# A second gated layer by seven block products instead of eight, with the output product moved behind it

## The chip, the cores and the metric

The kernel runs on one core of one Trainium2 chip. The metric is device time in microseconds (us). TensorE (PE, with its weight loads as PEld) multiplies into PSUM, which has eight banks here; VectorE (DVE) and ScalarE (ACT) read PSUM and work in SBUF; GpSimd (POOL) works in SBUF; SyncE (SP) issues DMAs.

## What is computed

```python
x = attention(q, k, v)                    # 2 x 768 tokens -> 1536 x 512
h = ((x @ moe_w1) * (x @ moe_w2)) @ moe_w3
y = h @ moe_w_out                         # 1536 x 512
a = y @ moe2_w_a                          # 512 x 1536
b = y @ moe2_w_b                          # 512 x 1536
return ((a * b) @ moe2_w_out).astype(np.float32)   # 1536 x 512
```

All inputs are float32 except the weights of both layers, which arrive as 64-bit floats and are turned into 32-bit ones on the chip.

## The kernel before

Tokens are the columns of the matmuls: 1536 tokens are three groups of `TG = 512`. Every 32-bit operand is held as two rounded parts (`fp32r`), hi and lo, and a product is three matmuls, lo·hi, hi·lo and hi·hi (`product`, L122 to L128, and `gate`, L679 to L681). A contraction of 512 is four chunks of 128, so a gate of one weight block and one token group is 12 matmuls into one PSUM bank.

The program is emitted by a generator, engine by engine, in the order of the text; nothing reorders it afterwards, and each engine works through its own queue in that order. Attention and the first layer's gates come first, mixed. Then `moe` (L693) makes y in twelve products of 24 matmuls (tags `y`, L736 to L756): three token groups of four row chunks each; ACT copies the hi part out of PSUM and DVE subtracts it for lo (`split_psum`, L77). At the same time ACT and DVE split the operands of the next group (`split_g`, L701).

The second layer's 1536 features are twelve blocks f of 128. For each f and token group, `gate` (L671) makes a and b in two banks (24 matmuls), ACT copies b out (L686), DVE multiplies (L687), and `split_sbuf` (L689) splits the result. The output product runs between the gates: features are taken in six groups of two, and `out_piece` (L765) multiplies a group's two blocks for one tile of 128 tokens (six matmuls) and adds the bank to an accumulator in SBUF (L786). The pieces of the last group follow the last gate; the last tile is done in two halves of 256 columns.

Weights come through `feed` (L180): SP loads a 512 KB block, ACT rewrites its two words (L94, L95), DVE joins them in three steps (L101, L105, L109), ACT rounds (L113), DVE subtracts (L117). Tiles come from pools with a fixed number of buffers (`unit` 34, `half` 8, `late` 11, PSUM `bank` 8), so a new tile waits for the last reader of the buffer that it takes.

Of the kernel before, what the change touches and what calls it, by code (L numbers as in the profile page):

```python
# [8 lines left out]
F32 = mybir.dt.float32  # L9
F32R = mybir.dt.float32r  # L10
I32 = mybir.dt.int32
# [3 lines left out]
ALU = mybir.AluOpType  # L15

P = 128
TG = 512
# [9 lines left out]
def f32(ap):  # L28
    return ap.bitcast(F32)


class Emitter:
# [48 lines left out]
    def convert(self, hi, lo, raw):  # L81
# [5 lines left out]
        g = self.half("g", list(hi.shape))  # L87
        gi = g.bitcast(I32)

        def words():  # L90

            nc.scalar.activation(out=g, in_=f32(high), func=AF.Copy, scale=WORD_SCALE)  # L94
            nc.scalar.activation(out=low, in_=low.bitcast(U32), func=AF.Copy, scale=2.0**-29)  # L95
            yield

        def join():


            nc.vector.tensor_scalar(  # L101
                out=gi, in0=gi, scalar1=0x0FFFFFFF, scalar2=3, op0=ALU.bitwise_and, op1=ALU.logical_shift_left
            )
# [6 lines left out]
            yield  # L110

        def upper():
# [18 lines left out]
    def weight_jobs(self):  # L131

        io, C = self.io, self.C
        nk = self.NF1
        wide, square = [P, 1, 2 * self.DM], [P, C, 2 * P]
        jobs = []
        for what, f, *_ in self.order:
            if what == "fold":
                for k in range(0, nk if f == 0 else 0, 2):
                    jobs.append((("wo", k), [(io["moe_w_out"][k + j].unsqueeze(1), wide) for j in range(2)]))  # L140
                jobs.append((("w3", f), [(io["moe_w3"][f][:, g : g + 4, :], square) for g in range(0, nk, 4)]))
            elif all(key != ("w12", f) for key, _ in jobs):
                jobs.append((("w12", f), [(io[n][f], square) for n in ("moe_w1", "moe_w2")]))
        for f in range(self.NF2):
            jobs.append((("wab", f), [(io[n][f], square) for n in ("moe2_w_a", "moe2_w_b")]))
            if f:
                jobs.append((("wo2", f - 1), [(io["moe2_w_out"][f - 1].unsqueeze(1), wide)]))
        jobs.append((("wo2", self.NF2 - 1), [(io["moe2_w_out"][self.NF2 - 1].unsqueeze(1), wide)]))
        return jobs

    def feed_start(self):
# [541 lines left out]
    def moe(self):  # L693

        nc, io = self.nc, self.io
        nf = self.NF1
# [1 line left out]
        g1 = [{} for _ in range(self.NTG)]  # L698
        gs = [[] for _ in range(self.NTG)]

        def split_g(tg, f):  # L701
            t = self.unit("gs", [P, 2, TG], F32R)
            self.split_sbuf(t, g1[tg].pop(f))
            gs[tg].append(t)

# [24 lines left out]
                    split_g(0, e)  # L730
            yield 1.3 * (at.stop - at.start) / TG

        self.lead = 6
        y = []
        nf2 = self.NF2
        for tg in range(self.NTG):  # L736
            ys = []
            for n in range(self.C):
                p = self.bank("y")
                cols = slice(n * P, (n + 1) * P)  # L740
                self.product(
# [3 lines left out]
                        for f in range(nf)  # L745
                    ],
                )
                t = self.act("y")
                self.split_psum(t[:, 0, :], t[:, 1, :], p)
                ys.append(t)  # L750
                if tg + 1 < self.NTG:
                    for f in range(2 * n, 2 * n + 2):
                        split_g(tg + 1, f)
                yield 5.2
            y.append(ys)
            gs[tg] = None  # L756
        self.wf = None

        ntt = self.NT // P
        acc = [self.late("acc", [P, 2, self.DM]) for _ in range(ntt // 2)]  # L760
        outs, g2 = {}, {}
        FG = 2
        groups = nf2 // FG

        def out_piece(grp, tt):  # L765
            for f in range(grp * FG, (grp + 1) * FG):
                if f not in outs:
                    outs[f] = self.need("wo2", f)[0]
            tg, o = divmod(tt * P, TG)
            a = acc[tt // 2][:, tt % 2, :]  # L770

            parts = 2 if (grp, tt) == (groups - 1, ntt - 1) else 1
            for n in range(parts):
                at = slice(n * self.DM // parts, (n + 1) * self.DM // parts)
                p = self.bank("o", (P, self.DM // parts))
                self.product(
                    p,
                    [
                        (g2[f][tg][:, 0, o : o + P], g2[f][tg][:, 1, o : o + P], outs[f][:, 0, 0, at], outs[f][:, 1, 0, at])
                        for f in range(grp * FG, (grp + 1) * FG)  # L780
                    ],
                )
                if grp == 0:
                    nc.vector.tensor_copy(out=a[:, at], in_=p)
                else:
                    nc.vector.tensor_tensor(out=a[:, at], in0=a[:, at], in1=p, op=ALU.add)  # L786
                if grp == groups - 1:
                    nc.sync.dma_start(io["out"][tt * P : (tt + 1) * P, at], a[:, at])

        for grp in range(groups):  # L790
            todo = [(grp - 1, tt) for tt in range(ntt)] if grp else []
            per = -(-ntt // (FG * self.NTG))
            for f in range(grp * FG, (grp + 1) * FG):
                g2[f] = []
                pair = self.need("wab", f)
                for tg in range(self.NTG):
                    g = self.half("gg", [P, TG])
                    yield from self.gate(pair, lambda c, tg=tg: (y[tg][c][:, 0, :], y[tg][c][:, 1, :]), g)
                    t = self.unit("g2", [P, 2, TG], F32R)
                    self.split_sbuf(t, g)  # L800
                    g2[f].append(t)
                    for _ in range(per):
                        if todo:
                            out_piece(*todo.pop(0))
                    yield 1.3
        for tt in range(ntt):
            out_piece(groups - 1, tt)
            yield 1.3

    def finish(self, work):  # L810
# [5 lines left out]
def tile_kernel(ctx, tc, io):  # L816
# [34 lines left out]
        e.hp, e.up = e.pool("hp", 8), e.pool("up", 34)  # L851
        return e

    def rest(e):
        e.lp = e.pool("lp", 11)

    with tc.If(narrow) as branch:
        with ExitStack() as arm, tc.manual_schedule():
# [6 lines left out]
            rest(e)  # L865
            e.finish(work)
    with branch.Else():
        with ExitStack() as arm, tc.manual_schedule():
            e = emitter(arm, "full")
            with ExitStack() as ctx:  # L870
                e.const, e.lp = e.pool("const", 1, ctx), e.pool("ap", 10, ctx)
                e.full_attention()
            rest(e)
            e.feed_start()
            e.finish(e.moe())

# [58 lines left out]
```

## Time and profile before

| | |
|---|---|
| three runs | 631.29, 632.20, 632.98 us; median 632.2 |
| profiled execution, first to last instruction | 631.2 us (its own time beyond this span is not listed) |
| PE busy | 614.2 us, 97% |
| DVE busy | 386.2 us, 61% |
| ACT busy | 299.1 us, 47% |
| POOL busy | 74.5 us, 12%, all of it in the first 130 us |
| chain that ended last | PE 87%, DVE 7%, ACT 2% |
| y products | from 267.2 us to 332.4 us |
| second layer's gates and the output product | from 332.4 us to 626.4 us |

Busy time is the time in which an engine had an instruction in flight; neighbouring matmuls overlap, so the distance from one start to the next, not the duration of one, is what a matmul costs. The chain follows the last instruction back through whatever released it.

### The profile page before, as it was taken

What the parts mean: (1) busy time and instruction counts of PE and PEld (TensorE: products, weight loads), DVE (VectorE), ACT (ScalarE), POOL (GpSimd) and SP (SyncE); (2) the same over time, 40 slices, a digit from 0 to 9 for tenths busy, and PEclk for the clock granted to TensorE, in tenths of its full rate; (3) what the DMA queues carried; (4) which work ended last, traced back from release to release, by engine and by line L of the source; (5) the groups of instructions that cost most, each with busy time, mean ns of one, the idle gap of its engine ahead of it and who ended that gap; (6) DMA issues with size and microseconds to landing.
All of it is one profiled execution on the core that took longest, in us unless ns stands there. A gap on an engine that the chain in (4) does not pass through costs nothing.

```text
span 631.2 us, 8920 instructions
## 1 busy us (share of the span) xinstructions
PE 614.2 (97%) x3230; PEld 512.0 (81%) x3230; DVE 386.2 (61%) x866; ACT 299.1 (47%) x655; POOL 74.5 (12%) x122
## 2 busy tenths in 40 slices
PE   6999999999999999999999999999999999999996
PEld 4688988888888888888888888888888888888885
DVE  6897989369874985823315566466566556553344
ACT  5898899656563774622314453153253243331110
POOL 5665667300000000000000000000000000000000
PEclk9899999999999999999999999999999999999999
DMA  8999772335331650100014011112112111000004
GB/s 233 270 256 210 174 195 68 135 126 174 106 128 34 199 175 25 69 1 0 1 36 165 33 34 67 67 66 68 68 66 67 67 67 66 1 0 1 0 35 171
DMA packets 20276, 58.86 MB, mean 93 GB/s; under 512 B 2688, under 2 KB 3456, under 8 KB 20224
## 3 DMA queue, kind: packets, MB, share of 16 engines
q1 hardware_dynamic: 19648, 57.42, 30.4%
q10 hardware_dynamic: 576, 0.79, 0.5%
q8 instruction: 27, 0.44, 0.3%
q14 instruction: 25, 0.20, 0.1%
HBM read 55.05 MB, written 3.15 MB: 92 GB/s over the span
## 4 chain that ended last, share of the span: by engine, by line
PE 87%; DVE 7%; ACT 2%; issue 2%; DMA 1%; POOL 1%; POOLq 0%; DVEq 0%; ACTq 0%
PE ab_band L679 16%; PE ab_band L681 16%; PE ab_band L680 16%; PE o_band L127 5%; PE o_band L128 5%; PE o_band L126 5%; PE y_band L128 3%; PE y_band L126 3%; PE y_band L127 3%; PE wfp_band L246 2%; PE wfp_band L248 2%; PE wfp_band L247 2%; PE pv_band L526 2%; DVE s_band L454 2%; PE pt_band L490 2%
## 5 line engine op out<-in xcount | busy, mean ns | idle before, releaser
L680 PE MATMUL ab_band<-y_band,w_band 128*128 128x512 f32 x288 | 112.0, 389 | 0.0
L679 PE MATMUL ab_band<-y_band,w_band 128*128 128x512 f32 x288 | 112.0, 389 | 0.0
L681 PE MATMUL ab_band<-y_band,w_band 128*128 128x512 f32 x288 | 112.0, 389 | 0.0
L686 ACT COPY b_band<-ab_band 128x512 f32<-128x512 f32 (+1 forms) x63 | 35.5, 566 | 150.7 <-PE ab_band L681 150.6
L679 PE MATMUL ab_band<-xh_band,w_band 128*128 128x512 f32 (+1 forms) x216 | 81.8, 379 | 0.0
L687 DVE TENSOR_TENSOR gg_band<-ab_band,b_band 128x512 f32<-128x512 f32 x36 | 24.9, 691 | 92.3 <-ACT b_band L686 92.3
L681 PE MATMUL ab_band<-xh_band,w_band 128*128 128x512 f32 (+1 forms) x216 | 79.0, 366 | 0.0
L680 PE MATMUL ab_band<-xl_band,w_band 128*128 128x512 f32 (+1 forms) x216 | 78.9, 365 | 0.0
L113 ACT CAST w_band<-g_band 128x512 fp32r<-128x512 f32 x76 | 47.3, 622 | 47.2 <-DVE g_band L109 45.0
L479 POOL TENSOR_SCALAR s_band<-s_band,z_band 128x256 f32<-128x256 f32 (+1 forms) x96 | 61.0, 648 | 37.1 <-DVE z_band L477 16.7
L679 PEld LDWEIGHTS ab_band<-y_band,w_band 128*128 128x128 f32 x288 | 54.1, 188 | 11.3
L680 PEld LDWEIGHTS ab_band<-y_band,w_band 128*128 128x128 f32 x288 | 54.1, 188 | 11.2
L681 PEld LDWEIGHTS ab_band<-y_band,w_band 128*128 128x128 f32 x288 | 54.1, 188 | 11.1
L109 DVE CUSTOM_DVE_ANT_0 g_band<-raw_band,g_band 128x1024 uint16<-128x1024 uint16 x76 | 52.9, 696 | 10.3 <-ACT raw_band L95 0.5
L127 PE MATMUL o_band<-w_band,g_band 128*128 128x512 f32 (+1 forms) x146 | 56.4, 386 | 0.0
L126 PE MATMUL o_band<-w_band,g_band 128*128 128x512 f32 (+1 forms) x146 | 56.4, 386 | 0.0
L128 PE MATMUL o_band<-w_band,g_band 128*128 128x512 f32 (+1 forms) x146 | 56.4, 386 | 0.0
L105 DVE SCALAR_TENSOR_TENSOR g_band<-raw_band,g_band 128x512 int32<-128x512 int32 x76 | 52.5, 691 | 2.3
L117 DVE TENSOR_TENSOR w_band<-g_band,w_band 128x512 fp32r<-128x512 f32 x76 | 51.2, 690 | 3.9 <-ACT w_band L113 3.5
L94 ACT ACTIVATE g_band<-raw_band 128x512 f32<-128x512 f32 x76 | 50.9, 670 | 0.0
L95 ACT ACTIVATE raw_band<-raw_band 128x512 int32<-128x512 uint32 x76 | 50.7, 668 | 0.0
L466 ACT ACTIVATE s_band<-s_band,m_band 128x256 f32<-128x256 f32 (+1 forms) x96 | 46.6, 492 | 3.5 <-DVE m_band L454 3.4
(89 smaller groups left out, 1036.0 us busy)
## 6 DMA issues: line engine op xcount, KB each, us to landing
raw_band<-in_moe_w_dram SPq DMA_DIRECT2D x31, 512.0 KB, 4.6
raw_band<-in_moe_w_out_dram SPq DMA_DIRECT2D x20, 512.0 KB, 4.2
raw_band<-in_moe_w_a_dram SPq DMA_DIRECT2D x12, 512.0 KB, 3.7
raw_band<-in_moe_w_b_dram SPq DMA_DIRECT2D x12, 512.0 KB, 3.7
v_band<-in_v_dram SPq DMA_DIRECT2D x12, 256.0 KB, 8.1
kd_band<-in_kq_dram SPq DMA_DIRECT2D x12, 256.0 KB, 7.5
qd_band<-in_kq_dram SPq DMA_DIRECT2D x12, 256.0 KB, 7.7
out_dram<-acc_band SPq DMA_DIRECT2D x11, 256.0 KB, 2.0
```

The source lines that it names most:

```text
L94: nc.scalar.activation(out=g, in_=f32(high), func=AF.Copy, scale=WORD_SCALE)
L95: nc.scalar.activation(out=low, in_=low.bitcast(U32), func=AF.Copy, scale=2.0**-29)
L105: nc.vector.scalar_tensor_tensor(out=gi, in0=high, scalar=-0x80000000, in1=gi, op0=ALU.bitwise_and, op1=ALU.bitwise_or)
L109: nc.vector.tensor_tensor(out=gi, in0=gi, in1=low, op=ALU.add)
L117: nc.vector.tensor_tensor(out=lo, in0=g, in1=f32(hi), op=ALU.subtract)
L126: self.nc.tensor.matmul(out, wl, xh, start=(i == 0), stop=False)
L127: self.nc.tensor.matmul(out, wh, xl, start=False, stop=False)
L128: self.nc.tensor.matmul(out, wh, xh, start=False, stop=(i == n - 1))
L479: nc.gpsimd.tensor_scalar(out=s[:, j, lo:], in0=s[:, j, lo:], scalar1=z[:, j : j + 1], scalar2=1.0, op0=ALU.mult, op1=ALU.mult)
L679: nc.tensor.matmul(p, wl, xh, start=(c == 0), stop=False)
L680: nc.tensor.matmul(p, wh, xl, start=False, stop=False)
L681: nc.tensor.matmul(p, wh, xh, start=False, stop=(c == self.C - 1))
```

## The change

The 2 x 2 blocks are: two halves of the contraction (256 each), the pair of weight blocks (w_a, w_b) of one f, and two halves of the tokens. Instead of eight block products of 256, seven are made (Strassen's algorithm in Winograd's form), from sums of weight blocks and sums of y blocks. Token groups 0 and 1 form one problem of 512 columns per half (q = 0), group 2 forms another of 256 columns per half (q = 1). One f is thus 14 products of six matmuls.

- `mixed` replaces the y loop: besides splitting y it makes the differences of y blocks on DVE and splits them too. It needs all 14 + 7 operand tiles in SBUF at once.
- `wab_load` and `wab_steps` replace `feed` for w_a and w_b: 15 steps per f that convert the pair, make four sums of 128 x 256 on POOL, and split 14 chunks. One step is emitted per product.
- `products` runs the twelve f. The sums over products are partly taken in PSUM: product 1 goes to bank z, ACT copies it out (p1), then product 6 is added to the same bank, ACT copies that (u2), then 5 and 3 are added; bank m takes 7 (copied, p7) and then 4; bank x takes 2. DVE adds the copies and multiplies a by b. `order0` is used at f = 0, `order` after it.
- The output product runs after all gates: eight token tiles accumulate over all twelve f in the eight PSUM banks, then the other four tiles run one at a time. The accumulators in SBUF and their additions are gone; ACT copies each finished tile.
- The pool `late` is closed after `mixed`, and two pools (`gp`, `tp`) take its place.

```diff
-        for f in range(self.NF2):
-            jobs.append((("wab", f), [(io[n][f], square) for n in ("moe2_w_a", "moe2_w_b")]))
...
+        ops = yield from self.mixed(gs, split_g)
+        self.wf = None
+        self.late_ctx.close()
+        self.lp = self.pool("gp", 8)
+        self.tp = self.pool("tp", 6)
+        yield from self.products(ops)
...
+    def wab_steps(self, f):
...
+        for words, _ in pairs:
+            for _ in words():
+                pass
+            yield
+        for _, join in pairs:
+            for _ in join():
+                yield
+        sf = self.late("sf", [P, 4, 2, P])
+        low, high = slice(0, 2), slice(2, 4)
+        add = lambda out, a, b, op: nc.gpsimd.tensor_tensor(out=out, in0=a, in1=b, op=op)
+        add(sf[:, 2], gb[:, low], gb[:, high], ALU.add)
+        add(sf[:, 1], ga[:, low], gb[:, low], ALU.subtract)
+        add(sf[:, 0], sf[:, 2], ga[:, low], ALU.subtract)
+        add(sf[:, 3], ga[:, high], sf[:, 0], ALU.subtract)
+        wa = self.unit("wa", [P, 2, C, P], F32R)
+        wd = self.half("wd", [P, 2, 2, P], F32R)
+        nc.scalar.copy(out=wa[:, 0], in_=ga)
+        nc.scalar.copy(out=wd[:, 0], in_=gb[:, high])
...
+                    sub(t[:, 1], p[:, H:], t[:, 0])
+                    sub(t[:, 2], p[:, H:], yb.pop(c)[:, H:])
+                    sub(t[:, 3], p[:, :H], t[:, 1])
+                    both = operand(p)
...
+                    self.split(th, tl, t)
...
+        order0 = [(0, 1), (0, 7), (0, 6), (0, 4), (1, 1), (0, 5), (1, 7), (0, 2), (1, 6), (1, 4), (0, 3), (1, 5), (1, 2), (1, 3)]
+        order = [(0, 1), (0, 7), (1, 1), (1, 7), (0, 6), (0, 4), (1, 6), (1, 4), (0, 5), (1, 5), (0, 2), (1, 2), (0, 3), (1, 3)]
...
+            for slot, (q, k) in enumerate(order if f else order0):
+                if k in (1, 7, 2):
+                    bank = self.bank("ab", (P, TG if q == 0 else H))
+                    {1: z, 7: m, 2: x}[k][q] = bank
+                bank = (m if k in (7, 4) else x if k == 2 else z)[q]
+                multiply(bank, w[k], ops[q][k], k in (1, 7, 2), True, k in (6, 5, 3, 4))
...
+                    if slot == 7:
+                        steps += [wo_steps(0), half_steps(ga, 0, halves)]
+                fill(steps)
...
+                if k == 1:
+                    p1[q] = temp("p1", q)
+                    copy(p1[q])
...
+            for tt in range(8):
+                if f == 0:
+                    banks[tt] = self.bank("o")
+                hi, lo = out_term(f, tt)
+                t = wo[f]
+                multiply(banks[tt], [(hi, lo)], [(t[:, 0, 0], t[:, 1, 0])], f == 0, f == nf2 - 1)
+                fill(steps)
```

The first place is ACT's queue where the y products end. `y` is an operand's hi part, `raw` a loaded weight block, `gb`/`ga` a pair of converted blocks, `p` the copy of product 1 or 7, `u` that of the sum of 1 and 6, `ab` a bank. Before:

```order
L78 CAST y_band_3620<-y_band_3595 128x512
L78 CAST y_band_3648<-y_band_3623 128x512
L78 CAST y_band_3676<-y_band_3651 128x512
L94 ACTIVATE g_band_3694<-raw_band_3171 128x512
L95 ACTIVATE raw_band_3171<-raw_band_3171 128x512
```

Now, with the line numbers of the changed kernel:

```order
L739 CAST y_band_3692<-y_band_3664 128x512 [waits DVE_49,PE_49]
L739 CAST y_band_3695<-tb_band_3618 128x1024
L89 ACTIVATE gb_band_3718<-raw_band_3707 128x512 [waits DMAHW1_49,Activation_49]
L90 ACTIVATE raw_band_3707<-raw_band_3707 128x512 [waits Activation_49]
L953 COPY p_band_3722<-ab_band_3711 128x512 [waits DVE_49,PE_49]
L89 ACTIVATE ga_band_3719<-raw_band_3708 128x512 [waits DMAHW2_49]
L90 ACTIVATE raw_band_3708<-raw_band_3708 128x512
L953 COPY p_band_3733<-ab_band_3724 128x512 [waits PE_49]
```

The copies of the first two bank contents (L953) stand behind two y casts and two pairs of word conversions, and the first of them also waits for DVE.

The second place is DVE's queue from the last gates into the output product (`gs` here is a split product a·b, `wo` a split output weight block, `ga`/`gb` the stored products of tokens 0 to 1023 and 1024 to 1535). Before, around the last gate:

```order
L687 TENSOR_TENSOR gg_band_5630<-ab_band_5631,b_band_5657 128x512
L691 TENSOR_TENSOR g_band_5660<-gg_band_5630,g_band_5660 128x512
L786 TENSOR_TENSOR acc_band_3684<-acc_band_3684,o_band_5663 128x512
L786 TENSOR_TENSOR acc_band_3684<-acc_band_3684,o_band_5671 128x512
L786 TENSOR_TENSOR acc_band_3679<-acc_band_3679,o_band_5679 128x512
```

Now:

```order
L119 TENSOR_TENSOR wo_band_5386<-g_band_5387,wo_band_5386 128x512 [waits Activation_49]
L972 TENSOR_TENSOR ga_band_5316<-ab_band_5317,p_band_5333 128x512 [waits PE_49]
L972 TENSOR_TENSOR gb_band_5174<-ab_band_5335,p_band_5351 128x256 [waits PE_49]
L905 TENSOR_TENSOR gs_band_5442<-ga_band_3706,gs_band_5441 128x1024 [waits Activation_49]
L94 TENSOR_SCALAR g_band_5453<-g_band_5453 128x512 [waits Activation_49]
```

The lo part of the first output operand (L905) stands behind the multiplication that reads the last gate product's bank. On PE, this is what the first output matmuls wait for:

```order
L913 MATMUL ab_band_5335<-y_band_3657,ws_band_5295 128x256 x2
L913 MATMUL ab_band_5335<-y_band_3692,ws_band_5295 128x256 x3
L913 MATMUL o_band_5448<-wo_band_5386,gs_band_5442 128x512 [waits DVE_49]
L913 MATMUL o_band_5448<-wo_band_5386,gs_band_5441 128x512 [waits Activation_49]
L913 MATMUL o_band_5448<-wo_band_5386,gs_band_5441 128x512
```

The first output matmul takes the lo part (`gs_band_5442`) and now follows the last gate matmul directly.

## Rows read from the trace of the kernel before

**Rows 1.** The page, first part: busy time, share of span, instructions.
```profile
PE 614.2 (97%) x3230; PEld 512.0 (81%) x3230; DVE 386.2 (61%) x866; ACT 299.1 (47%) x655; POOL 74.5 (12%) x122
```
**Rows 2.** Busy time by stretch: y products and before, then gates and output.
```profile
core 0: us, PE busy (x) PEld busy (x) DVE busy (x) ACT busy (x) POOL busy (x), PEclk, DMA share, GB/s
...
220.90:332.40 111.50, 111.50 (x493) 92.34 (x492) 53.02 (x86) 43.39 (x78) 0.00 (x0) 1.00 0.14 47
332.40:607.20 274.80, 274.80 (x1214) 227.52 (x1214) 153.34 (x249) 93.89 (x161) 0.00 (x0) 1.00 0.15 51
```
**Rows 3.** PE in order of time, 512 columns: start us, duration us, instruction.
```profile
399.76 0.39 PE L679 MATMUL ab_band<-y_band,w_band 128*128 128x512 f32 x1
...
405.88 0.39 PE L679 MATMUL ab_band<-y_band,w_band 128*128 128x512 f32 x1
```
**Rows 4.** PE in order of time, 256 columns: the last twelve matmuls.
```profile
624.84 0.28 PE L126 MATMUL o_band<-w_band,g_band 128*128 128x256 f32 x1
...
626.15 0.28 PE L128 MATMUL o_band<-w_band,g_band 128*128 128x256 f32 x1
```
**Rows 5.** Groups by line, PE and its weight loads: busy us, mean ns.
```profile
L679 PE MATMUL ab_band<-y_band,w_band 128*128 128x512 f32 x288 | 112.0, 389 | 0.0
```
```profile
L679 PEld LDWEIGHTS ab_band<-y_band,w_band 128*128 128x128 f32 x288 | 54.1, 188 | 11.3
```
**Rows 6.** Groups by line, DVE.
```profile
L109 DVE CUSTOM_DVE_ANT_0 g_band<-raw_band,g_band 128x1024 uint16<-128x1024 uint16 x76 | 52.9, 696 | 10.3 <-ACT raw_band L95 0.5
L105 DVE SCALAR_TENSOR_TENSOR g_band<-raw_band,g_band 128x512 int32<-128x512 int32 x76 | 52.5, 691 | 2.3
L117 DVE TENSOR_TENSOR w_band<-g_band,w_band 128x512 fp32r<-128x512 f32 x76 | 51.2, 690 | 3.9 <-ACT w_band L113 3.5
...
L101 DVE TENSOR_SCALAR g_band<-g_band 128x512 int32<-128x512 int32 x76 | 32.5, 428 | 1.7 <-ACT g_band L94 1.6
...
L393 DVE TENSOR_TENSOR qb_band<-qd_band,qa_band 128x1024 fp32r<-128x1024 f32 x6 | 7.2, 1202 | 0.0
...
L687 DVE TENSOR_TENSOR g_band<-ab_band,b_band 128x256 f32<-128x256 f32 x6 | 2.5, 418 | 6.8 <-ACT b_band L686 6.8
```
**Rows 7.** Groups by line, ACT.
```profile
L94 ACT ACTIVATE g_band<-raw_band 128x512 f32<-128x512 f32 x76 | 50.9, 670 | 0.0
...
L113 ACT CAST w_band<-g_band 128x512 fp32r<-128x512 f32 x76 | 47.3, 622 | 47.2 <-DVE g_band L109 45.0 <-DVE g_band L101 1.1 <-DVE wf_band L691 0.9
...
L686 ACT COPY b_band<-ab_band 128x512 f32<-128x512 f32 x57 | 33.3, 586 | 150.7 <-PE ab_band L681 150.6
...
L378 ACT CAST ks_band<-kd_band 128x1024 fp32r<-128x1024 f32 x6 | 6.3, 1051 | 0.0
...
L686 ACT COPY b_band<-ab_band 128x256 f32<-128x256 f32 x6 | 2.3, 378 | 0.0
```
**Rows 8.** ACT in order of time: two activations without a wait between them.
```profile
350.83 0.67 ACT L94 ACTIVATE g_band<-raw_band 128x512 f32<-128x512 f32 x1
351.40 0.67 ACT L95 ACTIVATE raw_band<-raw_band 128x512 int32<-128x512 uint32 x1
```
**Rows 9.** Single lines: durations ns min/median/max, first and last start us.
```profile
L479 POOL TENSOR_SCALAR s_band<-s_band,z_band x96: 366/479/1821, 10.8 to 118.4; 128x256 f32<-128x256 f32 x80, 128x128 f32<-128x128 f32 x16
```
```profile
L390 DVE TENSOR_TENSOR ks_band<-kd_band,ks_band x6: 1222/1399/1471, 51.8 to 99.4; 64x1024 fp32r<-64x1024 f32 x6
```
**Rows 10.** DVE in order of time: the first operation after the last matmul.
```profile
626.47 0.42 DVE L786 TENSOR_TENSOR acc_band<-acc_band,o_band 128x256 f32<-128x256 f32 x1 [0.30 <-PE o_band L128]
```
**Rows 11.** PE in order of time with its idle time, then PE by stretch with granted clock.
```profile
25.33 0.67 PE L526 MATMUL pv_band<-pt_band,v_band 128*64 128x128 f32 x8 [1.40 <-ACT pt_band L492]
```
```profile
26.50:27.00 0.50, 0.50 (x9) 0.50 1.00 217
...
29.50:30.00 0.50, 0.50 (x7) 0.70 1.08 307
```
**Rows 12.** DMA issues: KB each, median us from issue to landing.
```profile
raw_band<-in_moe_w_out_dram SPq DMA_DIRECT2D x20, 512.0 KB, 4.2
```

More of the change, by code (lines that the diff above doesn't have):

```diff
@@ L110, in join, with convert @@
             yield
+        return words, join
+    def convert(self, hi, lo, raw):
+        nc = self.nc
+        g = self.half("g", list(hi.shape))
+        words, join = self.doubles(g, raw)
         def upper():
@@ L736, in moe @@
         for tg in range(self.NTG):
-            ys = []
-            for n in range(self.C):
+            for n in range(C):
                 p = self.bank("y")
@@ new lines, in mixed @@
+                if tg == 0:
+                    nc.scalar.copy(out=(y21 if upper else y11)[:, c], in_=p)
+                    big[2 if upper else 1].append(operand(p))
+                elif tg == 1 and not upper:
+                    y12[c] = self.half("y12", [P, TG])
+                    nc.scalar.copy(out=y12[c], in_=p)
+                    sub(y11[:, c], p, y11[:, c])
+                    big[5].append(operand(y11[:, c]))
+                elif tg == 1:
+                    t2[c] = self.half("t2", [P, TG])
+                    big[3].append(operand(p))
+                    sub(t2[c], p, y11[:, c])
+                    sub(y12[c], p, y12[c])
+                    sub(y21[:, c], y21[:, c], t2[c])
+                    for k, t in ((7, y12.pop(c)), (6, t2.pop(c)), (4, y21[:, c])):
+                        big[k].append(operand(t))
+                elif not upper:
+                    if c == 0:
+                        first = self.unit("y", [P, 2, 2, H], F32R)
+                    yb[c] = self.half("yb", [P, TG])
+                    nc.scalar.copy(out=yb[c], in_=p)
+                    tb[c] = self.late("tb", [P, 4, H])
+                    sub(tb[c][:, 0], p[:, H:], yb[c][:, :H])
+                    self.split(first[:, c, 0], first[:, c, 1], p[:, :H])
+                    small[1].append((first[:, c, 0], first[:, c, 1]))
+                else:
+                    t = tb.pop(c)
+                    sub(t[:, 1], p[:, H:], t[:, 0])
+                    sub(t[:, 2], p[:, H:], yb.pop(c)[:, H:])
+                    sub(t[:, 3], p[:, :H], t[:, 1])
+                    both = operand(p)
+                    small[2].append(tuple(x[:, :H] for x in both))
+                    small[3].append(tuple(x[:, H:] for x in both))
+                    th, tl = (self.unit("y", [P, 4, H], F32R) for _ in range(2))
+                    self.split(th, tl, t)
+                    for e, k in enumerate((5, 6, 7, 4)):
+                        small[k].append((th[:, e], tl[:, e]))
@@ L754, in moe @@
+                if tg == 1 and n == C - 1:
+                    gs[tg] = None
+                    self.wab_load(0)
                 yield 5.2
-            y.append(ys)
             gs[tg] = None
-        self.wf = None
-        ntt = self.NT // P
[L760 to L772, printed above, removed]
+        for _ in weights:
+            pass
@@ L775, in out_piece @@
                 p = self.bank("o", (P, self.DM // parts))
[L776 to L807, printed above, removed]
+                terms = [out_term(f, tt) for f in range(nf2)]
+                multiply(p, terms, [(wo[f][:, 0, 0, at], wo[f][:, 1, 0, at]) for f in range(nf2)], True, True)
+                store(p, tt, at)
             yield 1.3
```

187 lines of the change are left out of this document (169 added, 18 removed).

## The prediction

> **What bounds the kernel now.** The first view is the page's busy time: PE works in 97% of the span, the next engine, DVE, in 61% [rows 1]. That is an average, so the second view is busy time by stretch: in the 111.5 us up to the end of the y products and in the 274.8 us of gates and output after them, PE has no idle time at all, at full granted clock, while DVE is busy for 153 of those 274.8 us and ACT for 94 [rows 2]. Whatever shortens PE's work there shortens the kernel, as long as PE is not made to wait. The third view is PE in order of time, since a duration of 389 ns [rows 5] is not what a matmul costs: 27 steps from 399.76 to 405.88 us [rows 3] make 0.2267 us per matmul of 512 columns, and 11 steps from 624.84 to 626.15 us [rows 4] make 0.1191 us for 256 columns. So half the columns cost 53%, and the weight load of 188 ns [rows 5], of which each of those twelve matmuls has one, hides even behind 0.119 us.
>
> **The change part by part.** *Gates.* Before: 12 blocks x 3 token groups x 24 = 864 matmuls of 512 columns, 864 x 0.2267 = 195.9 us. After: 14 products of 6 per block, half of them at 256 columns: 504 x 0.2267 + 504 x 0.1191 = 114.3 + 60.0 = 174.3 us. Gain 21.6 us, all on the path. The page "TensorE: Matmul & The Clock Gate" of the Trainium skill, section "Back-to-back issue gap", puts a warm matmul at columns / 2.4 GHz plus 2.5 ns; by it the gain would be an estimated 22.7 us. The rows show 13 ns beyond the columns at either width, so the smaller gain stands.
>
> *Output product.* Before: 71 pieces of 6 matmuls and two half pieces: 426 x 0.2267 + 12 x 0.1191 = 98.0 us. After: 8 tiles x 36 + 3 x 36 = 396 wide ones and 72 half ones: 98.4 us. Loss 0.4 us. The 74 additions into SBUF go; they lay beside PE's work and are worth nothing.
>
> *Y stage.* PE's 288 matmuls stay, 5.44 us per product. The heaviest product for DVE (group 1, upper half) now brings nine operations of 0.69 us [rows 6], 6.2 us, twice in a row; the next ones bring less, and the operands are needed 5 us later or more. I cost it at nothing. If that cover were gone it would be 2 x 0.8 us.
>
> *From y to gates.* Here PE must wait. After the last y product ACT and DVE in turn make the last operands (DVE three subtractions of 256 columns, 0.42 us each; ACT 0.59 and 1.05 us; DVE 1.20 us for 1024 columns [rows 6, 7]): 3 x 0.42 + 0.1 for hand-overs + 0.59 + 1.05 + 1.20 = 4.2 us, and only then may ACT copy product 1 out of bank z (its temporary takes the memory of a tile that DVE still reads), +0.59 = 4.8 us. Product 6, the third in `order0`, adds to that bank and so cannot start; without the wait it would start after two products, at 12 x 0.2267 = 2.72 us. Stall 2.1 us. Behind the copy stand two word conversions, 0.57 us apart [rows 8], and then the copy of product 7: 4.8 + 2 x 0.57 + 0.59 = 6.5 us, where product 4 wants its bank at 4.8 + 1.36 = 6.2 us: 0.3 us more. Together 2.4 us, once.
>
> *Inside a block.* Per f PE needs 42 x (0.2267 + 0.1191) = 14.5 us. DVE has two joins of three (3.6 us), 2.5 us of lo parts, five operations at 512 columns (3.5 us) and five at 256 (2.1 us): 11.7 us [rows 6]. ACT has 4 x 0.67 + 2.2 + 3 x 0.59 + 3 x 0.38 = 7.8 us [rows 7]. Each copy has two or three products, 2 us or more, before PE adds to its bank again. The longest chain: DVE's last join can only follow the addition of product 4 (PE at 6.9 us) and ends near 9.2 us; then two POOL sums of t each, ACT's 0.62 and DVE's 0.69 us, and PE needs the result in the second product of the next block, at 14.5 + 1.4 = 15.9 us. It holds for t up to 2.7 us. The trace has no POOL operation with two inputs. POOL with one input and mostly the same size took 0.37 to 1.82 us [rows 9]; I bound t by 0.37 us and, twice the longest, 3.6 us, and take twice the median, 1.0 us, since two operands are read instead of one and most rows lie near the median. Cost nothing. The transfers of the pair wait only for readers one block or more back, and 4.2 us each [rows 12] against 14.5 us hides them; without that cover the first product of a block would wait for them.
>
> *From gates to output.* The first output matmul needs a lo part of 1024 columns that stands on DVE behind the last gate's multiplication. The last matmul's result comes 0.16 us after PE's slot (0.28 - 0.12 [rows 4]), DVE starts 0.04 us later [rows 10], 0.42 + 1.20 us [rows 6], weight load 0.19 us [rows 5]: stall 2.0 us, once.
>
> *Output stage.* Per f PE needs 24 x 0.2267 = 5.44 us. The conversion of the next operands is a chain over ACT and DVE: joins 1.8, ACT rounding 0.62 and 1.05, DVE 1.20 us; with every second f 1.20 more. Two f: 4.7 + 5.9 = 10.6 us against PE's 10.9. I cost it at nothing, but the cover is 0.3 us.
>
> *End.* After the last matmul ACT's copy of 256 columns, 0.38 us, takes the place of DVE's 0.42 us [rows 7, 10]: nothing.
>
> *Clock.* PE's one idle gap of 1.40 us (before 25.33 us) was followed by a granted clock of 0.50, 1.2 instead of 2.4 GHz, from 26.5 to about 29.8 us [rows 11]. 3.3 us at half speed lose 1.6 us. The two stalls could each bring that, or nothing; no row shows such a gap in this part of the program. I take half of it, 1.6 us for both, and keep 0 and 3.2 for the range.
>
> **Sum.** -21.6 + 0.4 + 2.4 + 2.0 + 1.6 = -15.2 us on the profiled execution's span of 631.2 us; the median of the runs is 632.2, 1.0 us above that span, which I carry along: 617.0 us.
>
> **The rivals.**
> *No stall* (DVE and ACT overlap better than durations tell, and PE flows through both boundaries): 632.2 - 21.2 = 611.0 us. For it: successive ACT operations start 0.57 us apart at 0.67 us duration [rows 8]. Against it: both waits are chains across engines, where nothing overlaps.
> *The output stage's conversion becomes the bound*: 0.1 us more at each of some ten hand-overs per two f makes 11.6 us per pair against 10.9: six times 0.7, +4 us, 621 us.
> *POOL slows DVE.* While POOL worked, one DVE operation of the same size took 1222 to 1471 ns [rows 9], a factor of 1.20. DVE's 11.7 us per block become 14.0, just under PE's 14.5; with POOL's sums only part of the time it should hold, with a little more it costs about 0.5 us per block: +6 us, 623 us. The Trainium skill's "GPSIMD Engine Reference", section "Key points", says that GpSimd shares its SBUF interfaces with VectorE and collides with its instructions of two SBUF inputs, which speaks against these sums; the spread of 1222 to 1471 ns agrees.
> *Slower: POOL's sums set the pace.* In every block, ACT's rounding and DVE's lo part wait for POOL. Beyond t = 2.7 us each further us costs 2 us per block: the gain of 15.2 us is gone at 2.7 + 15.2/24 = 3.3 us per sum, and at 3.6 us the time is 617 + 12 x 1.8 = 639 us. For it: a 1.82 us row with one input. Against it: the median of 0.48 us.
> *The change does not do what it says*: the listed order shows 42 + 42 matmuls per block, so PE's work does fall; I give this nothing.
>
> **How the numbers follow.** About 0.3%, 1.9 us, is what a measurement of this kernel can tell from no change. Forecast (both stalls, clock from 0 to 3.2 us: 615.4 to 618.6) 0.53; no stall or a partial one (611 to 615) 0.20; output stage (619 to 622) 0.12; POOL slowing DVE (622 to 630) 0.10; POOL setting the pace 0.05, of which 0.04 is slower and 0.01 within 0.3%. So faster 0.94, same 0.02 (0.01 of it from the end of the contention case), slower 0.04. The range of 8 in 10 leaves out the POOL cases and a little below: 610.5 to 623.0 us.
>
> **What would show it.** Right: matmuls of 256 columns 0.119 us apart among those of 512; PE without idle time inside the blocks f = 1 to 11, 14.5 us each; two PE gaps, one of about 2.1 us two products after the last y product, ended by ACT's copy of product 1, one of about 2.0 us before the first output matmul, ended by DVE's lo part; POOL sums near 1 us. Wrong: PE idle within every block, ended by a cast of POOL's sums or by DVE; a row of equal waits in the output stage, ended by ACT or DVE conversions; a granted clock near 0.5 for longer than 3 us after a gap.

## The result, and the profile after

The kernel with the change takes 620.8 us (median of four runs, 619.4 to 622.1), the kernel before 631.9 us beside it: ratio 0.982, 95% interval 0.9802 to 0.9839, 11.1 us less. In a second series it was 620.5 against 631.9 us (0.9823, 0.9809 to 0.9836). The forecast was 617.0 us, 15.2 us less.

Busy times of the kernel after, from the page (before: [rows 1]):

```profile
PE 595.2 (96%) x3404; PEld 505.6 (82%) x3404; DVE 403.0 (65%) x907; ACT 333.6 (54%) x726; POOL 114.8 (19%) x170
```

Its busy time by stretch, as in [rows 2]: end of the y products, block f = 0, blocks 1 to 11, the step to the output, the output product.

```profile
core 0: us, PE busy (x) PEld busy (x) DVE busy (x) ACT busy (x) POOL busy (x), PEclk, DMA share, GB/s
220.00:331.05 111.05, 111.05 (x491) 91.96 (x490) 55.16 (x91) 44.60 (x82) 3.43 (x4) 1.00 0.07 24
331.05:350.24 19.19, 15.41 (x86) 12.80 (x84) 14.29 (x24) 9.74 (x18) 3.27 (x4) 1.00 0.24 83
350.24:511.50 161.26, 161.26 (x926) 141.96 (x924) 114.73 (x213) 76.41 (x150) 33.48 (x40) 1.00 0.21 71
511.50:513.85 2.35, 0.16 (x2) 0.00 (x1) 2.35 (x5) 0.24 (x1) 0.00 (x0) 1.00 0.68 228
513.85:612.40 98.55, 98.55 (x468) 83.03 (x468) 46.80 (x61) 41.27 (x60) 0.00 (x0) 1.00 0.17 60
```

Eleven blocks take 161.26 us, 14.66 us each, and PE never idles in them; the y products lost nothing either. All of PE's idle time between 220 and 612 us lies in the second and fourth stretch. What PE waited for, from 325 us on:

```profile
PE o_band L913 <- DVE gs_band L905: 2.2, 1, 2.2
PE ab_band L913 <- ACT p_band L953: 2.0, 1, 2.0
PE ab_band L913 <- DVE p_band L954: 1.8, 1, 1.8
```

The first two were forecast, the third was not. In PE's order of time (start, duration, instruction, idle before):

```profile
331.05 1.52 PE L913 MATMUL ab_band<-y_band,wa_band 128*128 128x512 f32 x6
332.41 1.52 PE L913 MATMUL ab_band<-y_band,ws_band 128*128 128x512 f32 x6
335.94 1.66 PE L913 MATMUL ab_band<-y_band,ws_band 128*128 128x512 f32 x6 [2.01 <-ACT p_band L953]
337.54 1.66 PE L913 MATMUL ab_band<-y_band,wd_band 128*128 128x512 f32 x6
339.03 0.88 PE L913 MATMUL ab_band<-y_band,wa_band 128*128 128x256 f32 x6
...
364.90 1.55 PE L913 MATMUL ab_band<-y_band,wa_band 128*128 128x512 f32 x6
366.29 1.52 PE L913 MATMUL ab_band<-y_band,ws_band 128*128 128x512 f32 x6
367.64 0.88 PE L913 MATMUL ab_band<-y_band,wa_band 128*128 128x256 f32 x6
...
379.56 1.55 PE L913 MATMUL ab_band<-y_band,wa_band 128*128 128x512 f32 x6
...
513.85 2.37 PE L913 MATMUL o_band<-wo_band,gs_band 128*128 128x512 f32 x9 [2.19 <-DVE gs_band L905]
```

The first product of a block (512 columns, after one of 256) takes 366.29 - 364.90 = 1.39 us, the next 1.35, where six matmuls by [rows 3] make 1.36. Five such changes per block make 0.15 us, about what a block is over its 14.52 us.

The two products after the first wait take 339.03 - 335.94 = 3.09 us instead of 2.72. The second of them, product 4, starts 0.24 us late, as ACT's copy of product 7 ends:

```profile
336.92 0.57 ACT L953 COPY p_band<-ab_band 128x512 f32<-128x512 f32 x1
```

The wait that was not forecast is DVE's. Its operations in f = 0:

```profile
344.16 1.25 DVE L970 TENSOR_TENSOR ga_band<-p_band,u_band 128x512 f32<-128x512 f32 x1
345.33 1.23 DVE L773 TENSOR_TENSOR wa_band<-ga_band,wa_band 128x512 fp32r<-128x512 f32 x1
...
347.75 1.28 DVE L781 TENSOR_TENSOR ws_band<-sf_band,ws_band 128x512 fp32r<-128x512 f32 x2
348.95 0.74 DVE L954 TENSOR_TENSOR p_band<-ab_band,p_band 128x256 f32<-128x256 f32 x2
```

The last row begins with the addition of product 5 of the half tokens, which frees the bank that the last product of the block adds to (the other addition in that row is product 2's). In `order0` that product 5 is twelfth, where the code also empties the queue of weight steps: the two lo parts at 347.75 stand ahead of the addition. They hold it back by 348.95 - 347.75 = 1.2 us. Without them it would by these rows have ended near 348.2 us, an estimate, and PE would have gone on at 347.5, so DVE was some 0.7 us late already. In the other blocks product 5 is tenth, and its addition comes first. About as much was lost in the two operations above: they took 1.25 and 1.23 us, where the same forms average 739 and 770 ns over all blocks. At that time POOL made its sums, whose groups are:

```profile
L763 POOL TENSOR_TENSOR sf_band<-ga_band,sf_band 128x256 f32<-128x256 f32 x11 | 11.8, 1069 | 0.9
L763 POOL TENSOR_TENSOR sf_band<-gb_band 128x256 f32<-128x256 f32 x11 | 9.1, 831 | 83.5 <-DVE gb_band L102 83.5
L763 POOL TENSOR_TENSOR sf_band<-sf_band,ga_band 128x256 f32<-128x256 f32 x11 | 8.2, 743 | 0.0
```

### The profile page after: what moved, and what is told of

Its sections match the earlier page's. It is cut to its first block, busy times and chain, and to the rows that moved or that the text cites. A ratio compares the mean times of both kernels' runs of the same rounds, so it can differ in the third digit from the quotient of the medians.

```text
span 617.2 us, 9497 instructions
## 1 busy us (share of the span) xinstructions
PE 595.2 (96%) x3404; PEld 505.6 (82%) x3404; DVE 403.0 (65%) x907; ACT 333.6 (54%) x726; POOL 114.8 (19%) x170
## 4 chain that ended last, share of the span: by engine, by line
PE 82%; DVE 7%; DMA 7%; issue 1%; SPq 1%; ACT 1%; ACTq 0%; DVEq 0%
PE ab_band L913 27%; PE o_band L913 16%; PE ab_band L676 6%; PE ab_band L677 6%; PE ab_band L678 6%; PE y_band L128 4%; PE y_band L129 4%; PE y_band L130 4%; DMA qd_band<-in_kq_dram 2%; PE wfp_band L244 2%; PE wfp_band L243 2%; PE wfp_band L245 2%; PE pv_band L523 2%; DMA kq_band<-in_kq_dram 2%; DMA raw_band<-in_moe_w_dram 2%
## 5 line engine op out<-in xcount | busy, mean ns | idle before, releaser
L913 PE MATMUL ab_band<-y_band,ws_band 128*128 128x512 f32 (+1 forms) x576 | 110.7, 338 | 3.8 <-ACT p_band L953 2.0
L913 PEld LDWEIGHTS ab_band<-y_band,ws_band 128*128 128x128 f32 x576 | 91.1, 190 | 16.5 <-ACT p_band L953 2.4
L913 PE MATMUL o_band<-wo_band,gs_band 128*128 128x512 f32 (+1 forms) x468 | 98.7, 373 | 2.2 <-DVE gs_band L905 2.2
L913 PEld LDWEIGHTS o_band<-wo_band,gs_band 128*128 128x128 f32 x468 | 83.0, 188 | 17.9 <-DVE gs_band L905 2.4
L476 POOL TENSOR_SCALAR s_band<-s_band,z_band 128x256 f32<-128x256 f32 (+1 forms) x96 | 61.0, 648 | 36.0 <-DVE z_band L474 16.8
L913 PE MATMUL ab_band<-y_band,wa_band 128*128 128x512 f32 (+1 forms) x288 | 56.4, 338 | 0.0
L913 PEld LDWEIGHTS ab_band<-y_band,wa_band 128*128 128x128 f32 x288 | 46.0, 190 | 6.1
L676 PEld LDWEIGHTS ab_band<-xh_band,w_band 128*128 128x128 f32 x216 | 40.7, 188 | 7.6 <-issue 1.0
L678 PEld LDWEIGHTS ab_band<-xh_band,w_band 128*128 128x128 f32 x216 | 40.6, 188 | 6.7
L677 PEld LDWEIGHTS ab_band<-xl_band,w_band 128*128 128x128 f32 x216 | 40.7, 189 | 6.0
L953 ACT COPY p_band<-ab_band 128x512 f32<-128x512 f32 (+1 forms) x48 | 21.9, 480 | 39.1 <-PE ab_band L913 38.8
L451 DVE CUSTOM_DVE_ANT_0 s_band<-sp_band,bias_band 128x256 f32<-128x256 f32 (+1 forms) x96 | 37.1, 388 | 0.6 <-ACT bias_band L316 0.4
L130 PE MATMUL y_band<-gs_band,wf_band 128*128 128x512 f32 x96 | 37.4, 389 | 0.0
```

What stands on the lines that cost most here:

```text
L130: self.nc.tensor.matmul(out, wh, xh, start=False, stop=(i == n - 1))
L451: nc.vector.tensor_tensor_reduce(out=s[:, j, lo:], in0=sp[:, j, lo:], in1=bias[:, 2 * c + j, :], scale=-self.scale, scalar=FLT_MAX, op0=AL ...
L476: nc.gpsimd.tensor_scalar(out=s[:, j, lo:], in0=s[:, j, lo:], scalar1=z[:, j : j + 1], scalar2=1.0, op0=ALU.mult, op1=ALU.mult)
L676: nc.tensor.matmul(p, wl, xh, start=(c == 0), stop=False)
L677: nc.tensor.matmul(p, wh, xl, start=False, stop=False)
L678: nc.tensor.matmul(p, wh, xh, start=False, stop=(c == self.C - 1))
```

## The experiments

Theory W: what the kernel loses beside its matmuls are one-time waits at the edges of the gate stage, two of them forecast, and 0.14 us per block. Rivals: the granted clock (C), POOL's contention with DVE or its pace, and that the blocks are not bound by PE at all. The experiments ran on four chips, on which the kernel before took 631.9 us (the first four runs), 632.7 (the next four), 633.0 (POOL's sums twice and the first grouped order) and 632.6 us (the last two), so a difference between chips is good to about 1 us.

**The change again**, for its clock beside the others.

> The changed kernel once more, beside the experiments of this call, to have its time and its clock on the same chip. Theory W (waits): the missing 4 us of the forecast are one-time waits of PE at the edges of the gate stage (2.0 us and two slow copies at the start of f = 0, 1.8 us at the end of f = 0, 2.2 us before the output) and 0.14 us per block; then about 620.8 us again, with the same three waits in the profile. Rival C (clock): the granted clock falls after these waits in most runs and costs more than the waits do; then runs of this kernel differ by 2 to 3 us in step with their mean clock (0.990 to 0.998), those of the kernel before do not.

620.5 us, the same three waits of 2.0, 1.8 and 2.2 us. The spans of five runs were 616.8, 619.1, 618.1, 618.3 and 619.6 us at mean clocks of 0.999, 0.990, 0.995, 0.996 and 0.993; the kernel before had 629.5 to 631.0 us at 1.000 to 0.995. At a clock of 0.999 or more the two differ by 629.5 - 616.8 = 12.7 us, in the medians of the spans by 630.1 - 618.3 = 11.8. So the clock cost the change some 0.9 us more than the kernel before. Another 0.35 us lies outside the span: a run takes 1.8 us more than its span before, 2.1 to 2.2 us after, and 1.8 to 2.2 us in the versions below (why is open).

**The start of f = 0, first try.**

```
-        self.lp = self.pool("gp", 8)
         self.tp = self.pool("tp", 6)
+        self.lp = self.pool("gp", 8)
...
-                fill(steps)
+                early = f == 0 and slot < 2
+                if not early:
+                    fill(steps)
```

> Two edits at the start of f = 0: the temporaries take other memory (not that of a tile that DVE still reads), and the word conversions of the next block's weights begin two products later, behind ACT's copies of products 1 and 7. W: ACT's copy of product 1 can start at the end of its last cast, about 1.3 us sooner, so PE's first wait falls from 2.0 to about 0.7 us, and the following two products come at 1.36 us instead of 1.6 and 1.5: the profiled span falls by about 1.7 us, if DVE's wait at the end of f = 0 does not take it back (it may: DVE was late there, so 0 to 1.7). C: the span hardly changes while a gap of any length stays; the clock decides.

Slower: 623.6 us. ACT and PE in the order of time, one row and four:

```profile
336.24 1.07 ACT L955 COPY p_band<-ab_band 128x512 f32<-128x512 f32 x2 [1.34 <-DVE y_band L740]
```
```profile
336.88 2.20 PE L913 MATMUL ab_band<-y_band,ws_band 128*128 128x512 f32 x6 [2.01 <-ACT p_band L955]
338.88 2.61 PE L913 MATMUL ab_band<-y_band,wd_band 128*128 128x512 f32 x6
341.33 0.86 PE L913 MATMUL ab_band<-y_band,wa_band 128*128 128x256 f32 x6
...
353.09 0.98 PE L913 MATMUL ab_band<-y_band,ws_band 128*128 128x256 f32 x6 [3.16 <-DVE p_band L956]
```

The copy still waits for DVE's lo part, though the pool of its temporary is now the first to be opened in the memory that the closed pool leaves. Later word conversions only made DVE later: 3.2 us at the end of f = 0. And two products took 4.45 us instead of 2.72, at a granted clock of 0.62 in that stretch.

**The step to the output.**

```
+                    if slot == 1:
+                        steps.append(half_steps(ga, 0, halves))
                     if slot == 7:
-                        steps += [wo_steps(0), half_steps(ga, 0, halves)]
+                        steps.append(wo_steps(0))
```

> One edit in the last block: the split of the first output operand (ga of f = 0, finished long ago) begins in its second product instead of its eighth, and before the conversion of the first output weights. W: the 2.2 us that PE waits before the first output matmul go entirely, -2.0 to -2.2 us, about 618.7 us. No-gain rival: the wait moves to the banks (eight output banks must come free, DVE's last multiplication reads two of them), then 0.5 to 1 us stays. C: more than 2.2 us goes, since the clock dip behind the gap goes too (3 us or more).

618.2 us, 2.3 less. The first output matmul no longer waits; PE waits 0.2 us for DVE once, 6 us later, before the second block of the output product (rows under the second try with this step). That term of the forecast is right in place, cause and size.

**These edits together**, and in f = 0 the queue of weight steps is emptied after the addition of product 5.

```
+                if f == 0 and slot == 11:
+                    flush()
```

> The edits of e_first and e_half, and in f = 0 DVE adds product 5 of the half tokens to its temporary before it makes the last two lo parts of the next weights, instead of after. W: first wait 2.0 to 0.7, two slow copies 0.4 to 0, the wait at the end of f = 0 from 1.8 to 0.6, the one before the output 2.2 to 0: -5.0 us together, about 615.8 us. C: beyond that up to 2 us more, about 614, with the mean clock of all runs at 0.998. If the edges were not what the forecast missed: 619 to 621 us.

617.2 us, where 615.8 was expected: the output's wait went, the one at the end of f = 0 fell to 1.1 us, the first stayed, and the clock fell behind it. PE in order of time, then two stretches:

```profile
335.38 2.69 PE L913 MATMUL ab_band<-y_band,ws_band 128*128 128x512 f32 x6 [2.01 <-ACT p_band L960]
337.87 2.13 PE L913 MATMUL ab_band<-y_band,wd_band 128*128 128x512 f32 x6
339.84 0.87 PE L913 MATMUL ab_band<-y_band,wa_band 128*128 128x256 f32 x6
```
```profile
335.38:339.84 4.46, 4.46 (x12) 3.53 (x13) 0.00 (x0) 3.27 (x6) 0.00 (x0) 0.62 0.00 0
339.84:347.00 7.16, 7.16 (x45) 6.38 (x44) 5.94 (x11) 1.12 (x3) 0.76 (x1) 1.00 0.30 82
```

4.46 us for two products instead of 2.72. The profile of the change had the same wait of 2.0 us at the same place and no fall, and took 3.09 us for them: one fall of the clock costs 1.4 to 1.7 us.

**The start of f = 0, second try**: temporaries from a pool that was never closed, product 1 of the half tokens third, words after the copies, both joins before the first addition (DVE idled 5.4 us there in the first try), and the queue emptied after the addition of product 5.

```
+            if f == 0 and q == 0:
+                return self.half(name, [P, TG])
...
-        order0 = [(0, 1), (0, 7), (0, 6), (0, 4), (1, 1), (0, 5), (1, 7), (0, 2), (1, 6), (1, 4), (0, 3), (1, 5), (1, 2), (1, 3)]
+        order0 = [(0, 1), (0, 7), (1, 1), (0, 6), (0, 4), (0, 5), (1, 7), (0, 2), (1, 6), (1, 4), (0, 3), (1, 5), (1, 2), (1, 3)]
...
-                fill(steps)
+                if f:
+                    fill(steps)
...
+                if f == 0 and slot:
+                    for _ in range(4 if slot in (2, 3) else 1):
+                        fill(steps)
+                    if slot == 11:
+                        flush()
```

> The start of f = 0 once more, since the other memory pool left the copy waiting for the same DVE operation: the three wide temporaries of f = 0 come from the pool of half buffers, whose last readers are long done; the first product of the half tokens moves to third place, so that PE has 0.7 us more to do before it needs the copy; the word conversions follow the copies, and both joins of the next weights run before the first addition, in the 5.4 us in which DVE was idle. W: PE's first wait (2.0 us, with the low clock after it) and the one at the end of f = 0 (1.8 us) both go, the one before the output (2.2 us) stays: span 616.8 - 2.0 - 0.4 - 1.8 = 612.6 us, time about 614.8 us plus what the clock loses after the last wait (0 to 1.5 us). C, now as a part of W: the low clock after the first wait cost 1.7 us in the run with all edits and was absent in the profile of the changed kernel; without that wait the clock stays at 1.00 up to the output and the runs lie within 1.5 us of each other. Rival D: DVE is late in f = 0 whatever the order, and a wait of 1 us or more stays at its end.

617.0 us, 3.5 less than the change and 0.7 above the expected 614.8 to 616.3; span of the profiled run 613.2. Both waits of f = 0 are gone but for 0.4 us, and rival D falls. The part on the clock failed: the runs spread over 2.6 us at mean clocks of 0.993 to 0.999.

**Second try and output step together.**

> The edits of e_edge and of e_half together: no wait at any edge of the gate stage is left but 0.2 us before the output. W: 620.5 - 2.4 - 1.8 - 2.0 = 614.3 us by the waits alone; with the 1 to 2 us that the low clock costs in most runs, 612.5 to 613.5 us, all runs at a mean clock of 0.998 or more and within 1 us. If the clock falls for another reason than these waits: 614 to 615.5 us with clocks of 0.990 to 0.997.

614.9 us (614.4 to 615.0), ratio 0.9719 (0.9706 to 0.9733), the fastest version; a second series gave 614.7. Its stretches f = 0 and f = 1 to 11, the waits that are left, the first output matmuls, and ACT's copies of products 1 and 7, which now follow its cast at once:

```profile
331.77:347.50 15.73, 15.32 (x85) 12.94 (x84) 13.67 (x24) 9.37 (x18) 3.51 (x4) 1.00 0.31 104
347.50:508.76 161.26, 161.26 (x926) 142.03 (x925) 116.11 (x215) 76.58 (x150) 33.48 (x40) 1.00 0.22 71
```
```profile
PE ab_band L915 <- ACT u_band L962: 0.4, 1, 0.4
PE o_band L915 <- DVE gs_band L907: 0.2, 1, 0.2
```
```profile
508.76 5.79 PE L915 MATMUL o_band<-wo_band,gs_band 128*128 128x512 f32 x24
514.74 5.51 PE L915 MATMUL o_band<-wo_band,gs_band 128*128 128x512 f32 x23 [0.18 <-DVE gs_band L907]
```
```profile
333.63 1.05 ACT L739 CAST y_band<-tb_band 128x1024 fp32r<-128x1024 f32 x1
334.58 1.07 ACT L962 COPY p_band<-ab_band 128x512 f32<-128x512 f32 x2
```

f = 0 went from 19.19 to 15.73 us, the waits around the output's start from 2.2 to 0.2: 5.5 us, of 5.6 us between the two medians (6.5 us with each set against the kernel before on its own chip). That is the 614.3 us of the waits alone to about 1 us, and the 612.5 to 613.5 us that counted on a higher clock did not come. So C is not the main cause: the mean clock of these runs is still 0.995 to 0.997, and in the profiled one the fall lies at 26 to 30 us, long before the change.

**Product 1 of every block twice.**

```
-                multiply(bank, w[k], ops[q][k], ...
+                for _ in range(2 if k == 1 else 1):
+                    multiply(bank, w[k], ops[q][k], ...
```

> Every block computes its product 1 twice (the second overwrites the first), eight products per half as the plain method would need. PE-bound theory: 12 x 6 x (0.2267 + 0.1191) = 24.9 us more of matmuls; the first wait of f = 0 shrinks by about 1.2 us and the one at its end by about 1.3, since PE comes later: 642 to 645 us, slower than before the change (631.9). Rival (blocks are set by DVE's or POOL's chain and PE has slack): less than 15 us more, blocks well below 14.66 + 2.07 = 16.73 us.

644.7 us, ratio 1.0188 (1.0171 to 1.0206) to the kernel before. A block is 382.72 - 365.98 = 16.74 us by PE's rows:

```profile
365.98 2.26 PE L913 MATMUL ab_band<-y_band,wa_band 128*128 128x512 f32 x12
...
382.72 2.26 PE L913 MATMUL ab_band<-y_band,wa_band 128*128 128x512 f32 x12
```

One product more costs its 2.07 us in each block. So PE bounds the blocks, and with eight products the new form would be slower than the old.

**POOL's sums on DVE.**

```
-        add = lambda ...: nc.gpsimd.tensor_tensor(...
+        add = lambda ...: nc.vector.tensor_tensor(...
```

> The four sums of weights per block on DVE instead of POOL. PE-bound theory: blocks stay at 14.66 us (DVE goes from about 11.7 to 13.4 us of them), and the time within 1 us of 620.5 us; without POOL the DVE operations of 512 columns that took 1.2 us beside POOL's sums take 0.69 us. Contention rival (POOL slows DVE and that is what was lost): the wait at the end of f = 0 falls by 0.5 us or more and the blocks get shorter. The other way: DVE becomes the bound at some place of the block, blocks above 15 us, 625 us or more.

620.1 us; waits of 2.0, 2.1 and 2.2 us, and blocks of 395.40 - 380.74 = 14.66 us still:

```profile
380.74 1.55 PE L913 MATMUL ab_band<-y_band,wa_band 128*128 128x512 f32 x6
...
395.40 1.55 PE L913 MATMUL ab_band<-y_band,wa_band 128*128 128x512 f32 x6
```

DVE has room for the sums in a block, and taking POOL's contention away wins nothing, since DVE then makes the sums in the same place of f = 0.

**POOL's sums twice.**

```
+        for _ in range(2):
+            add(sf[:, 2], gb[:, low], gb[:, high], ALU.add)
...
```

> On top of the change as made (620.5 us): POOL makes the four sums of each block twice, the second time over the first. Working of the prediction: the chain over POOL's sums holds until they take 2.7 us each, and twice 0.85 is 1.7; so the blocks f = 1 to 11 stay at 14.66 us. Only f = 0 pays, where DVE's last two lo parts wait for the sums and stand ahead of an addition that PE needs: its wait of 1.8 us becomes about 5 us, the time about 624 us. Rival P (POOL is near to setting the pace): every block stretches, by 0.5 us or more, 630 us or more.

627.3 us. PE's rows at the end of f = 0 and at the starts of f = 2 and 3:

```profile
353.65 1.09 PE L914 MATMUL ab_band<-y_band,ws_band 128*128 128x256 f32 x6 [3.62 <-DVE p_band L955]
...
370.72 1.55 PE L914 MATMUL ab_band<-y_band,wa_band 128*128 128x512 f32 x6
...
385.49 1.55 PE L914 MATMUL ab_band<-y_band,wa_band 128*128 128x512 f32 x6
```

The wait of f = 0 grew by 1.8 us (to 3.6, not to the expected 5), and blocks by 0.11 to 14.77 us: the second product comes late now. Between ga's last join and the first cast of sums lie six sums instead of two, some 5.4 us, and the forecast's limit was 2 x 2.7 = 5.4: right to a tenth. These make 3.0 us of the 6.7 (5.6 with each set against the kernel before on its own chip); the expectation of 624 us missed the rest, which goes with mean clocks of 0.985 to 0.991. The profiled run shows a mean granted clock of 0.66 to 0.79 in the 5 to 8 us around and behind each of its three waits.

**Products of one width together.**

```
-        order = [(0, 1), (0, 7), (1, 1), (1, 7), (0, 6), (0, 4), (1, 6), (1, 4), (0, 5), (1, 5), (0, 2), (1, 2), (0, 3), (1, 3)]
+        order = [(0, 1), (0, 7), (0, 6), (0, 4), (1, 1), (1, 7), (1, 6), (1, 4), (0, 5), (0, 2), (0, 3), (1, 5), (1, 2), (1, 3)]
```

In the first two slots of these blocks the weight steps also follow the copies.

> On top of the version without edge waits (614.9 us): in the blocks f = 1 to 11 the products of the same width stand together (four of 512 columns, four of 256, three of 512, three of 256), so that PE goes from 256 to 512 columns twice per block instead of five times. Theory S: the 0.14 us by which a block is longer than its matmuls is 24 ns at each such change, most of it; then a block takes 14.58 us instead of 14.66 and the time falls by about 0.8 us, to 614.1. Rival: the 0.14 us has another source (waits of single matmuls); blocks stay at 14.66 us. Risk: copies and additions have less time between two products of the same bank; a wait in every block would show as blocks above 14.8 us and 617 us or more.

627.9 us: the risk came true. PE's waits, and its rows at the end of a block:

```profile
PE ab_band L915 <- DVE p_band L963: 11.0, 10, 1.2
```
```profile
375.64 0.88 PE L915 MATMUL ab_band<-y_band,wa_band 128*128 128x256 f32 x6
377.71 0.98 PE L915 MATMUL ab_band<-y_band,ws_band 128*128 128x256 f32 x6 [1.19 <-DVE p_band L963]
378.53 1.55 PE L915 MATMUL ab_band<-y_band,wa_band 128*128 128x512 f32 x6
```

In this order product 5 of the half tokens is twelfth in every block, and the wait of f = 0 came back, 1.2 us in each of blocks 1 to 9: the same queue on DVE, shown a second time. Blocks 10 and 11 have no queue to empty there; block 10 shows no wait and block 11 one of 0.3 us. So the queue was emptied after the addition in all blocks:

```
-                if f and slot == 11 and f + 2 < nf2:
-                    flush()
...
+                if slot == 11 and f + 2 < nf2:
+                    flush()
```

> The grouped order once more, with its new wait taken out: in every block DVE makes the last two lo parts of the next weights after it has added product 5 of the half tokens, not before (as in f = 0). Theory S: the steps of PE in the grouped run, without its wait of 1.2 us per block, add up to 14.59 us; if DVE's addition now comes in time, blocks are 14.6 us and the time is 0.8 us under the version without edge waits, about 614.1 us. If the addition still comes late by 0.1 us or more per block, the gain is gone: 615 to 616 us.

> The version without edge waits again, on the chip of the grouped order, to compare the two: 614.9 us, blocks 14.66 us.

616.7 us against 614.7 of the version without edge waits on the same chip, where 615 to 616 us was the expectation for a late addition. Blocks are 377.23 - 362.39 = 14.84 us:

```profile
362.39 1.55 PE L915 MATMUL ab_band<-y_band,wa_band 128*128 128x512 f32 x6
...
377.23 1.55 PE L915 MATMUL ab_band<-y_band,wa_band 128*128 128x512 f32 x6
```

The addition still ends 0.14 us late, and the product that waits for it starts 0.1 us slower. The changes of width cost what theory S says (twice 1.39 instead of 1.36 us, 14.6 us for the rest), but the order that saves them gives more back.

## Why the forecast was right, and where it was not

- **What bounds it: right.** PE idles in none of the blocks 1 to 11, and one product more per block costs exactly its matmuls.
- **Gates, -21.6: mis-sized by 1.6.** 12 x 14.66 = 175.9 us instead of 174.3. The step that failed is taking 0.2267 and 0.1191 us from stretches of one width: 24 to 30 ns are lost where 512 columns follow 256. The Trainium skill's "TensorE: Matmul & The Clock Gate", section "Back-to-back issue gap", gives the form that led to the estimated 22.7 us for an isolated matmul, not for a stream with a weight load each, which the prediction left out; the trace gives 20.0, so the rows were nearer.
- **Output +0.4, end 0, y stage 0: right.** The output product takes 98.55 us instead of 98.4, without a wait behind its first matmul, so the rival of the output stage falls (without the wait before it, 0.2 us of that rival show once); PE is busy for all 111.05 us up to the first gate.
- **y to gates, +2.4: right.** 2.0 us idle and 0.4 us in the next two products. The causes were right too: with memory from a pool that was never closed the copy starts behind its cast at once, and product 4 starts just as the copy of product 7 ends.
- **Inside a block, 0: right for f = 1 to 11, wrong for f = 0.** The step that failed is "inside a block": it was worked out for `order` and carried over to `order0`, where an addition that PE needs stands behind two lo parts on a DVE that is late already. 1.8 us, with the slower start after it 2.1.
- **Gates to output, +2.0: right** (2.2, all of it gone with the earlier split).
- **POOL: right.** Sums took 0.74 to 1.07 us for the 1.0 taken. The Trainium skill's "GPSIMD Engine Reference", section "Key points", warns of the collision with VectorE; DVE's 1.25 us beside POOL for a form that averages 0.74 agrees, but with the sums on DVE the time was the same.
- **Clock, +1.6: about right for the changed kernel, too much as a difference.** In the profiled run nothing; over the runs of one series the median span lies 618.3 - 616.8 = 1.5 us above the one at full clock, but that of the kernel before lies 0.6 above its own.
- **The basis: two errors that nearly cancel, which is luck.** The profiled run of before held a fall of the clock at its start [rows 11]: 631.2 us, where the span at full clock is 629.5, so 1.7 us too much. And 1.0 us was carried between span and median, where a run of the change takes 2.2 us more than its span, so 1.2 us too little.

The sum without the clock was -21.6 + 0.4 + 2.4 + 2.0 = -16.8 us; at full clock the spans differ by -12.7. The 4.1 us between them are 1.6 of the gates, 2.1 at the end of f = 0, 0.2 before the output and 0.2 of the output product. They put the time of 620.8 us above the forecast's own band of 615.4 to 618.6 us and into that of the output-stage rival, which is not what happened; the wide range held it.

## What to carry to other kernels

A step that takes work from the bound engine moves its cost to the edges of the stage: work out the first block and the last by themselves, with their own order, since a chain that fits in the steady block need not fit in the first. For each result that the bound engine waits for, read what stands ahead of it in its own engine's queue; here one addition behind two conversions was late by 1.2 us for them alone, once, and made PE wait 1.2 us in each of nine blocks in another order. And if temporaries take the memory of a closed pool, ask who read that pool last.

## What the runs showed that was not expected

- The granted clock need not fall after a wait of PE. Waits of 2.0, 1.8 and 2.2 us left it at 1.00 in two profiles of the change; the same 2.0 us was followed by 0.62 over some 4.4 us in the first try, with the output step and with these edits together; and in the first try it stayed at 1.00 after 3.2 us. The length of the wait alone does not tell. One fall cost 1.4 to 1.7 us. The Trainium skill's "TensorE: Matmul & The Clock Gate", section "What's actually happening", says that the hardware's watch on PE's activity runs free of the kernel's start; that one kernel shows both agrees with it, and no run here tests it.
- Six matmuls of 512 columns take 1.39 us after 256 columns and 1.36 after 512, in every block.
- A DVE operation of 128x512 with two SBUF operands took up to 1.25 us beside POOL's sums and 0.69 us as a rule [rows 6].
